# Softmax weights that go through memory undivided, with their reciprocals as a tenth block

## The chip, the cores and the metric

The kernel runs on one core of one Trainium2 chip. The metric is the device time of one execution in microseconds. Engines are named as in the profile: PE (TensorE, matmuls), PEld (its weight loads), DVE (VectorE), ACT (ScalarE), POOL (GpSimd), SP (SyncE, which here issues all DMAs). A step below is one turn of the kernel's main loop.

## The reference

Attention with 8 batches, 8 heads, 576 rows and a head width of 64, all f32, in which each row keeps only its 32 largest scores, followed by a layer with a hidden width of 2048:

```python
scores = scale * np.matmul(q, k.transpose(0, 1, 3, 2))
kth = np.partition(scores, -top_k, axis=-1)[..., -top_k:-top_k + 1]
scores = np.where(scores >= kth, scores, -1000000000.0)
scores = scores - np.max(scores, axis=-1, keepdims=True)
attn = np.exp(scores)
attn = attn / (np.sum(attn, axis=-1, keepdims=True) + 1e-09)
x = np.matmul(attn, v)              # then heads side by side: (4608, 512)
h = x @ w_in                        # (4608, 2048)
g = np.where(h >= 1, h, np.where(h <= -1, 0.0, (h + 1) ** 2 / 4))
out = g @ w_out                     # (4608, 512)
```

## The kernel before, in words

A step takes two heads (a head pair `hp`) of one block `t` of 128 queries: rows of 576 scores for each head, 128 queries on the partitions. 576 is four blocks of 128 (NT = 4) and a tail of 64; the tail queries of two heads fill one step (`t == NT`). There are 144 steps, 128 of them with `t < NT` and 16 tails. Four steps (two for tails, of two batches together) fill a chunk of 128 rows of x, held transposed in `xT` (128 x 4 x 128, one part for each head pair), and each of the 36 chunks goes through the hidden layer.

What a step does:

- `scores` (L329): PE multiplies queries and keys into PSUM (`sp`), ACT copies them to `s` with the scale (L348).
- `first_top` and `weights` (L371, L406): DVE finds the 32nd largest of each row. It works on the larger of each pair of columns (`more`) and the smaller (`less`, both L361), with rounds of max8 and match_replace (L368, L381, L409 and so on), and merges the two lists with a scan (L440). ACT takes exponentials of all scores (L384). At the end DVE zeroes the exponentials below the threshold and sums the rest (L447: out e, sums z).
- `divide` (L391), at the start of the next step: DVE takes the reciprocals of z (L393). Then either (`by_tensor`, in the first 9 steps and the last two) ACT makes diagonal matrices of them (L397), or POOL multiplies the 128 x 576 weights of each head by them (L400).
- The weights must be transposed for the value product. `by_tensor` steps do it on PE (`transpose_w`, L456). The other 133 go through memory (`move_w`, L473): ACT sorts the f32 weights into their upper and lower 16-bit halves (L477, two copies), SP writes them to DRAM (L479, `rows`) and then issues a DMA transpose back into `wT` (L480), which is 9 blocks of 128 x 128: four for each head and one with both tails. SP's transpose waits until the rows have landed.
- `values` (L486), two steps later: PE multiplies values and `wT` into the PSUM tile `po` (L494, L502 for tails), and ACT copies it into the step's part of `xT` (L507, L509).
- When the last part of a chunk is there, `mlp` (L518) queues its work: 8 groups `hidden` (L521; each 8 products `ph`, L527, of which every fourth reads `xT[:, 3]`; then ACT L531 and L538, then POOL L543, L544, L545), and 16 products `final` (L547; `py`, L550), each group's four groups behind it. The output `y` is copied by ACT (L553) and written (L555).

Keys and queries of the later batches are transposed in the same way as weights, by ACT (`turn`, L272), a write to DRAM (L274, `lines`) and a DMA transpose (L275). ACT also inspects the loaded weights of the layer in odd steps (L168).

What sets the order: PE, DVE, ACT and POOL carry out their instructions in the order in which the loop (L723) emits them. Each step has 7 slots. The division of the step before is emitted in slot 0, `transpose_w` of the step before in slot 1, the value product of the step two before in slot 2, followed by the scores of the step two ahead; `move_w` of the step before comes in slot 3. After every slot `advance` (L621) takes queued work of the layer by a planner's cost, so that each step gets an even share of it. SP's order is not in that list; the framework sets it.

Buffers that matter here: `halves` has one buffer, `wT` three, `ph` and `po` share three in PSUM, `r` has two, `g` eight, the queries `q_in` two and the tail queries `q_tl` one.

Of the kernel before, what the change touches and what calls it, by code (L numbers as in the profile page):

```python
# [11 lines left out]
F32 = mybir.dt.float32  # L12
U16 = mybir.dt.uint16
# [3 lines left out]
ALU = mybir.AluOpType  # L17
# [8 lines left out]
def kernel(  # L26
# [10 lines left out]
    nc = tc.nc  # L37
    B, H, S, D = q.shape
    NTOK, DM = out.shape
    DFF = moe_w_in.shape[1]  # L40
    P = 128
# [4 lines left out]
    NT = S // P  # L46
    SM = NT * P
    TL = S - SM
    assert 2 * TL == P
    SH = S // 2  # L50
    BLOCKS = 2 * NT + 1
# [120 lines left out]
    def run(ctx, paired):  # L172
        xtp = ctx.enter_context(tc.tile_pool(name="xtp", bufs=6))
        stage = ctx.enter_context(tc.tile_pool(name="stage", bufs=2))
        att = ctx.enter_context(tc.tile_pool(name="att", bufs=2))
        dram = ctx.enter_context(tc.tile_pool(name="dram", bufs=3, space=bass.MemoryType.DRAM))
# [3 lines left out]
        def whole(x, b):  # L180

            return x[b, :, 0:SM, :].rearrange("h (p c) d -> p h c d", c=NT)
# [17 lines left out]
        def load_queries(b, t):  # L200
            if t < NT:
                q_in = stage.tile([P, H, D], F32, name="q_in", bufs=2)
                nc.sync.dma_start(out=q_in, in_=whole(q, b)[:, :, t, :])
            else:
                q_in = stage.tile([TL, H, D], F32, name="q_tl", bufs=1)
                nc.sync.dma_start(out=q_in, in_=q[b, :, SM:S, :].rearrange("h p d -> p h d"))
            return q_in


        def main(i):  # L210
            return slice(0, SM) if i == 0 else slice(TL, S)

        def tail(i):
            return slice(SM, S) if i == 0 else slice(0, TL)

        def part(i, j):
            return slice(0, TL) if i == j else slice(TL, P)
# [171 lines left out]
                st["rest"] = att.tile([P, 2, S], F32, name="rest", bufs=1)  # L389

        def divide(st):  # L391
            rz = att.tile([P, 2], F32, name="rz")
            nc.vector.reciprocal(rz, st["z"])  # L393
            if st["by_tensor"]:
                st["rz"] = diag = (late or words).tile([P, 2, P], F32, name="diag", tag="halves", bufs=1)
                for i in range(2):
                    nc.scalar.activation(diag[:, i, :], ident, AF.Copy, scale=rz[:, i:i + 1])  # L397
            else:
                for i in range(2):
                    nc.gpsimd.tensor_scalar(st["e"][:, i, :], st["e"][:, i, :], rz[:, i:i + 1], 1.0, ALU.mult, ALU.mult)  # L400
            if paired:
                m, seconds, kth = st["m"], st["seconds"], st["kth"]
                nc.gpsimd.tensor_tensor(out=excess[:, 2 * m:2 * m + 2], in0=seconds[:, 8:9 + SPLIT:SPLIT], in1=kth[:, LAST:7:-SPLIT],
                                        op=ALU.subtract)

        def weights(st, before, after):  # L406
            m, tops = st["m"], st["tops"]
            for x in largest(st, 8):
                x()  # L409
                if before is not None:  # L410
                    divide(before)
                    before = None
# [38 lines left out]
            if after is None:  # L451
                divide(st)
# [2 lines left out]

        def transpose_w(st):  # L456
            w = st["e"]
            st["wT"] = wT = (late or words).tile([P, BLOCKS, P], F32, name="wT", bufs=3 if late else 1)
            pt = ps.tile([P, 2, NT, P], F32, name="pw", tag="a", bufs=2)
            for i in range(2):  # L460
                for c in range(NT):
                    nc.tensor.matmul(pt[:, i, c, :], w[:, i, main(i)][:, c * P:(c + 1) * P], st["rz"][:, i, :],  # L462
                                     start=True, stop=True)
            for i in range(2):
                nc.scalar.copy(wT[:, i * (NT + 1):i * (NT + 1) + NT], pt[:, i])
            pt = ps.tile([P, P], F32, name="pwt", tag="a", bufs=2)
            for i in range(2):
                nc.tensor.matmul(pt[i * TL:(i + 1) * TL, :], w[:, i, tail(i)], st["rz"][:, i, :], start=True, stop=True)
            nc.scalar.copy(wT[:, NT], pt)
# [1 line left out]


        def move_w(st):  # L473
            st["wT"] = wT = late.tile([P, BLOCKS, P], F32, name="wT", bufs=3)
            halves = late.tile([P, 2, 2 * S], U16, name="halves")
            for i in range(2):
                nc.scalar.copy(halves[:, :, i * S:(i + 1) * S], st["e"][:, i, :].bitcast(U16).rearrange("p (k t) -> p t k", t=2))  # L477
            rows = dram.tile([P, 2, 2 * S], U16, name="rows")
            nc.sync.dma_start(out=rows, in_=halves)  # L479
            nc.sync.dma_start_transpose(wT.bitcast(U16), rows.rearrange("p t k -> (p t) k"))  # L480

        def block(i, c):
            return i * (NT + 1) + c if c < NT else NT


        def values(st):  # L486
            t, hp, v_in, v_tl = st["t"], st["hp"], st["keys"]["v"], st["keys"]["v_tl"]
            wT = st["wT"]
            po = ps.tile([P, P], F32, name="po", tag="ph", bufs=3)
            if t < NT:  # L490
                for c in range(NT + 1):
                    for j in range(2):
                        h = 2 * hp + j
                        nc.tensor.matmul(po[j * D:(j + 1) * D], v_in[:, h, c, :] if c < NT else v_tl[0][:, h, :],  # L494
                                         wT[:, block(j, c)], start=(c == 0), stop=(c == NT))
            else:
                for i in range(2):
                    cols = slice(i * TL, (i + 1) * TL)
                    for c in range(NT + 1):
                        for j in range(2):  # L500
                            h = 2 * (hp + i) + j
                            nc.tensor.matmul(po[j * D:(j + 1) * D, cols], v_in[:, h, c, :] if c < NT else v_tl[1][:, h, :],  # L502
                                             wT[:, block(i, c), part(i, j)],
                                             start=(c == 0), stop=(c == NT))
            xT, col = st["xT"]
            if t < NT:
                nc.scalar.copy(xT[:, hp, col:col + P], po)  # L507
            else:
                nc.scalar.copy(xT[:, hp:hp + 2, col:col + TL], po.rearrange("p (i n) -> p i n", i=2))  # L509

# [68 lines left out]
        for b, t in rounds:  # L579
            tile_of = (b, t) if t < NT else (b - b % 2, t)  # L580
            ch = chunks.index(tile_of)
            col = TL if t == NT and b % 2 else 0
            for hp in (range(NHP) if t < NT else range(0, NHP, 2)):
                steps.append((b, t, hp, ch, col))
        n = len(steps)
# [5 lines left out]
        words, late = conversion.enter_context(tc.tile_pool(name="words", bufs=1)), None  # L591
# [53 lines left out]
        def fetch(i):  # L645
            if i < len(rounds) and rounds[i] not in q_ins:
                q_ins[rounds[i]] = load_queries(*rounds[i])
# [63 lines left out]
        def values_until(m):  # L711
            nonlocal valued, pe_time
            while valued < min(m, n):
                pe_time = max(pe_time, ready_at[valued]) + 1.25
                values(state[valued])
                state[valued] = None
                if valued in ready:
                    ch = ready[valued]
                    mlp(xTs[ch], rows_of(*chunks[ch]), mlp_pool, ch == len(chunks) - 1)
                valued += 1  # L720

        first_late = None
        for m in range(n + 2):  # L723
# [3 lines left out]
            elif not early and late is None:  # L727
                conversion.close()
                room.clear()
                late = ctx.enter_context(tc.tile_pool(name="late", bufs=1))  # L730
# [15 lines left out]
            for slot in range(SLOTS):  # L746
# [11 lines left out]
                if slot == 1 and 1 <= m <= n and state[m - 1]["by_tensor"]:  # L758
                    pe_time = max(pe_time, done[m - 1] + 2.0) + 1.0
                    transpose_w(state[m - 1])  # L760
                    ready_at[m - 1] = pe_time + 1.8
                if slot == 3 and 1 <= m <= n and state[m - 1] is not None and not state[m - 1]["by_tensor"]:
                    move_w(state[m - 1])
                    ready_at[m - 1] = done[m - 1] + 15.0
# [75 lines left out]
```

## Time and profile before

| | |
|---|---|
| median of 3 runs (lowest to highest) | 1533.05 us (1530.18 to 1536.14) |
| the profiled execution | 1536.15 us |
| its span, first to last instruction | 1534.3 us |
| granted TensorE clock, mean | 0.979 |
| POOL L400, the division: 266 instructions | 250.2 us busy, 951 ns each |
| ACT L477, the halves: 266 instructions | 293.6 us busy, 1144 ns each |
| DVE L447, threshold and sum: 288 instructions | 267.3 us busy, 962 ns each |
| rows to DRAM, 133 times 576 KB | 3.2 us from issue to landing |
| transpose of the rows, 133 times | 5.0 us from issue to landing |
| DMA share, mean rate | 64.7% of 16 engines, 169 GB/s |

In the lines of the profile, a group or a row of the timeline has engine, line, operation and tiles (out<-in). A line of waits has the waiting instruction, what released it, the sum in us, how many times, and the longest. In the timeline the first two numbers are the start (us from the span's start) and the length; `[0.90 <-ACT g L538]` says that the engine was idle for 0.90 us before it, until ACT's L538 released it. Times in the table by stage are busy times of the engines, which overlap.

### The profile page before, as it was taken

What the parts mean: (1) busy time and instruction counts of PE and PEld (TensorE: products, weight loads), DVE (VectorE), ACT (ScalarE), POOL (GpSimd) and SP (SyncE); (2) the same over time, 40 slices, a digit from 0 to 9 for tenths busy, and PEclk for the clock granted to TensorE, in tenths of its full rate; (3) what the DMA queues carried; (4) which work ended last, traced back from release to release, by engine and by line L of the source; (5) the groups of instructions that cost most, each with busy time, mean ns of one, the idle gap of its engine ahead of it and who ended that gap; (6) DMA issues with size and microseconds to landing.
All of it is one profiled execution on the core that took longest, in us unless ns stands there. A gap on an engine that the chain in (4) does not pass through costs nothing.

```text
span 1534.3 us, 32263 instructions
## 1 busy us (share of the span) xinstructions
PE 1452.4 (95%) x10625; PEld 1043.3 (68%) x10625; DVE 1445.1 (94%) x4443; ACT 1160.6 (76%) x2269; POOL 977.1 (64%) x1382
## 2 busy tenths in 40 slices
PE   5587999999999999999999999999999999999998
PEld 3465677677777767677777777676676677777675
DVE  6998999999999999999999999999999999999912
ACT  5776877877778888788778887787777888777732
POOL 4887556666666666566666666666666666666630
PEclk7788999999999999999999999999999999999999
DMA  8532467875676866986677877886577767565410
GB/s 241 158 116 81 121 167 157 214 190 158 165 196 183 214 171 180 217 215 179 165 196 185 202 176 186 212 204 178 155 182 193 197 167 191 156 160 157 134 39 17
DMA packets 512450, 259.78 MB, mean 169 GB/s; under 512 B 459152, under 2 KB 467344, under 8 KB 512272
## 3 DMA queue, kind: packets, MB, share of 16 engines
q1 hardware_dynamic: 512272, 257.62, 64.7%
q8 instruction: 86, 1.41, 0.4%
q14 instruction: 92, 0.75, 0.2%
HBM read 62.91 MB, written 102.04 MB: 108 GB/s over the span
## 4 chain that ended last, share of the span: by engine, by line
PE 79%; ACT 6%; DVE 6%; DMA 5%; issue 2%; POOL 1%; SPq 0%; DVEq 0%; ACTq 0%; POOLq 0%
PE py L550 30%; PE ph L527 28%; PE sp L347 9%; PE po L494 9%; DMA wT<-rows 2%; ACT halves L477 2%; DMA rows<-halves 2%; ACT e L384 1%; PE po L502 1%; DVE more L368 1%; DVE bits L148 1%; DVE e L447 1%; ACT raw L168 1%; PE pw L462 1%; ACT s L348 1%
## 5 line engine op out<-in xcount | busy, mean ns | idle before, releaser
L527 PEld LDWEIGHTS ph<-xT,w_in 128*128 128x128 f32 x4608 | 549.0, 193 | 102.8 <-issue 82.6
L527 PE MATMUL ph<-xT,w_in 128*128 128x128 f32 x4608 | 559.1, 277 | 4.5 <-POOL w_in L161 4.5
L550 PE MATMUL py<-w_out,g 128*128 128x512 f32 x1152 | 551.3, 603 | 0.0
L543 POOL TENSOR_SCALAR r<-r 128x256 f32<-128x256 f32 x276 | 152.1, 551 | 432.0 <-ACT r L531 431.9
L368 DVE MATCH_REPLACE8 more<-tops,more 128x288 f32<-128x288 f32 x864 | 374.9, 437 | 0.0
L550 PEld LDWEIGHTS py<-w_out,g 128*128 128x128 f32 x1152 | 198.5, 191 | 182.0 <-issue 161.8
L477 ACT COPY halves<-e 128x1152 uint16<-128x1152 uint16 x266 | 293.6, 1144 | 17.7 <-POOL e L400 8.3
L447 DVE SCALAR_TENSOR_TENSOR e<-s,kth,e 128x577 f32<-128x577 f32 x288 | 267.3, 962 | 1.8 <-ACT e L384 1.6
L545 POOL TENSOR_TENSOR g<-r,g 128x256 f32<-128x256 f32 x280 | 244.3, 873 | 22.0
L400 POOL TENSOR_SCALAR e<-e,rz 128x576 f32<-128x576 f32 x266 | 250.2, 951 | 3.6 <-DVE rz L393 3.6
L531 ACT ACTIVATE r<-ph,half 128x256 f32<-128x256 f32 (+1 forms) x296 | 136.4, 461 | 121.3 <-PE ph L527 84.4
L384 ACT ACTIVATE e<-s,nmax 128x576 f32<-128x576 f32 x288 | 222.7, 774 | 4.7
L348 ACT ACTIVATE s<-sp 128x576 f32<-128x576 f32 x288 | 172.6, 653 | 47.2 <-PE sp L347 45.2
L544 POOL TENSOR_TENSOR r<-r 128x256 f32<-128x256 f32 x276 | 190.7, 691 | 23.0
L347 PE MATMUL sp<-kT,qT 64*128 64x288 f32 x1024 | 163.8, 437 | 11.9 <-ACT kT L250 11.0
L494 PEld LDWEIGHTS po<-wT,v_in 128*64 128x64 f32 x2048 | 111.3, 137 | 83.3 <-ACT g L538 33.7
L494 PE MATMUL po<-wT,v_in 128*64 128x128 f32 x2048 | 143.6, 280 | 20.4 <-DMA wT<-rows 10.6
L538 ACT ACTIVATE g<-ph,minus 128x256 f32<-128x256 f32 x280 | 130.5, 466 | 0.0
L361 DVE TENSOR_TENSOR less<-s 128x576 f32<-128x576 f32 x144 | 125.9, 874 | 0.0
L409 DVE MAX8 tops<-more 128x8 f32<-128x288 f32 x288 | 125.4, 443 | 0.0
L347 PEld LDWEIGHTS sp<-kT,qT 64*128 64x128 f32 x1024 | 90.2, 189 | 48.1 <-issue 15.6
L361 DVE TENSOR_TENSOR more<-s 128x576 f32<-128x576 f32 x144 | 112.6, 782 | 6.7 <-ACT s L348 6.7
(91 smaller groups left out, 1423.6 us busy)
## 6 DMA issues: line engine op xcount, KB each, us to landing
rows<-halves SPq DMA_DIRECT2D x133, 576.0 KB, 3.2
lines<-parts SPq DMA_DIRECT2D x48, 256.0 KB, 2.8
q_in<-in_q_dram SPq DMA_DIRECT2D x32, 256.0 KB, 4.3
kT<-in_moe_w_in_dram SPq DMA_DIRECT2D x32, 256.0 KB, 3.3
v_in<-in_moe_w_out_dram SPq DMA_DIRECT2D x32, 256.0 KB, 3.0
v_in<-in_v_dram SPq DMA_DIRECT2D x32, 256.0 KB, 4.1
raw<-in_moe_w_in_dram SPq DMA_DIRECT2D x32, 256.0 KB, 3.1
out_dram<-y SPq DMA_DIRECT2D x32, 256.0 KB, 3.1
```

Source lines behind the costliest of these rows:

```text
L347: nc.tensor.matmul(*x, start=True, stop=True)
L361: nc.vector.tensor_tensor(out=x, in0=s[:, :, 0:SH], in1=s[:, :, SH:S], op=op)
L368: nc.vector.match_replace(out=st["rest"][:, i, :], in_to_replace=eight(st["tops"], i, r - 8), in_values=src[:, i, :], imm_value=LOWEST)
L384: nc.scalar.activation(e[:, i, :], s[:, i, :], AF.Exp, bias=nmax[:, i:i + 1])
L400: nc.gpsimd.tensor_scalar(st["e"][:, i, :], st["e"][:, i, :], rz[:, i:i + 1], 1.0, ALU.mult, ALU.mult)
L447: nc.vector.scalar_tensor_tensor(out=st["all"][1][:, i, :], in0=st["all"][0][:, i, :], scalar=last[i], in1=st["all"][1][:, i, :], op0=ALU. ...
L477: nc.scalar.copy(halves[:, :, i * S:(i + 1) * S], st["e"][:, i, :].bitcast(U16).rearrange("p (k t) -> p t k", t=2))
L494: nc.tensor.matmul(po[j * D:(j + 1) * D], v_in[:, h, c, :] if c < NT else v_tl[0][:, h, :], wT[:, block(j, c)], start=(c == 0), stop=(c == ...
L527: nc.tensor.matmul(ph[:, i], w_in[:, kk, f * P:(f + 1) * P], xT[:, kk], start=(kk == 0), stop=(kk == NK - 1))
L544: nc.gpsimd.tensor_tensor(out=r, in0=r, in1=r, op=ALU.mult)
L545: nc.gpsimd.tensor_tensor(out=g, in0=r, in1=g, op=ALU.add)
L550: nc.tensor.matmul(py[0], gs[f // group][:, f % group], w_out[:, f, :], start=(f == 0), stop=(f == NF - 1))
```

## The change

The weights of the 117 steps that go through memory and are no tails are not divided before they go. Instead their two reciprocals a row, spread over 64 columns each, are appended as 128 more columns; they come back transposed as a tenth block of `wT`, in which the upper 64 partitions hold the reciprocals of one head and the lower 64 those of the other, one column for each query. That is the layout of the value product, and POOL multiplies the part of `xT` by that block, after ACT has copied it from PSUM. Tails are divided as before; their rows are as long as before, but lie in tiles with room for 128 more columns.

`rz` gets three buffers, since it is read a step later than before. `wT` and `halves` grow. The tail queries share the two buffers of the other queries.

```diff
                 q_in = stage.tile([P, H, D], F32, name="q_in", bufs=2)
...
-                q_in = stage.tile([TL, H, D], F32, name="q_tl", bufs=1)
+                q_in = stage.tile([TL, H, D], F32, name="q_tl", tag="q_in", bufs=2)
...
         def divide(st):
-            rz = att.tile([P, 2], F32, name="rz")
+            rz = att.tile([P, 2], F32, name="rz", bufs=3)
             nc.vector.reciprocal(rz, st["z"])
             if st["by_tensor"]:
...
+            elif st["t"] < NT:
+                st["rz"] = rz
             else:
                 for i in range(2):
                     nc.gpsimd.tensor_scalar(st["e"][:, i, :], st["e"][:, i, :], rz[:, i:i + 1], 1.0, ALU.mult, ALU.mult)
...
         def move_w(st):
-            st["wT"] = wT = late.tile([P, BLOCKS, P], F32, name="wT", bufs=3)
-            halves = late.tile([P, 2, 2 * S], U16, name="halves")
+            st["wT"] = wT = late.tile([P, BLOCKS + 1, P], F32, name="wT", bufs=3)
+            halves = late.tile([P, 2, 2 * S + P], U16, name="halves")
             for i in range(2):
                 nc.scalar.copy(halves[:, :, i * S:(i + 1) * S], st["e"][:, i, :].bitcast(U16).rearrange("p (k t) -> p t k", t=2))
-            rows = dram.tile([P, 2, 2 * S], U16, name="rows")
-            nc.sync.dma_start(out=rows, in_=halves)
-            nc.sync.dma_start_transpose(wT.bitcast(U16), rows.rearrange("p t k -> (p t) k"))
+            n = 2 * S
+            if st["t"] < NT:
+                n += P
+                nc.scalar.copy(halves[:, :, 2 * S:n].rearrange("p t (i d) -> p t i d", d=D),
+                               st["rz"].bitcast(U16).rearrange("p (i t) -> p t i", t=2).unsqueeze(3).to_broadcast([P, 2, 2, D]))
+            rows = dram.tile([P, 2, 2 * S + P], U16, name="rows")
+            nc.sync.dma_start(out=rows[:, :, 0:n], in_=halves[:, :, 0:n])
+            nc.sync.dma_start_transpose(wT[:, 0:n // P].bitcast(U16), rows[:, :, 0:n].rearrange("p t k -> (p t) k"))
...
             if t < NT:
                 nc.scalar.copy(xT[:, hp, col:col + P], po)
+                if not st["by_tensor"]:
+                    x = xT[:, hp, col:col + P]
+                    nc.gpsimd.tensor_tensor(out=x, in0=x, in1=wT[:, BLOCKS, :], op=ALU.mult)
```

## The prediction

> **What bounds the kernel now.** I read four views: the page's busy times, busy time by stage, the waits of PE and of DVE from 200 to 1463 us, and the timeline around two places where PE meets the changed work.
>
> First the page, then the stages (columns: us, then busy time of PE, PEld, DVE, ACT, POOL, the granted clock, DMA share, GB/s):
>
> ```profile
> PE 1452.4 (95%) x10625; PEld 1043.3 (68%) x10625; DVE 1445.1 (94%) x4443; ACT 1160.6 (76%) x2269; POOL 977.1 (64%) x1382
> ```
> ```profile
> 200.00:400.00 200.00, 196.00 (x1530) 141.99 (x1527) 200.00 (x620) 156.48 (x302) 129.43 (x182) 1.00 0.70 179
> ...
> 1000.00:1200.00 200.00, 195.46 (x1387) 139.73 (x1386) 194.88 (x608) 157.61 (x300) 130.07 (x180) 1.00 0.70 182
> 1200.00:1400.00 200.00, 199.64 (x1544) 141.90 (x1543) 199.01 (x618) 159.70 (x308) 134.05 (x187) 1.00 0.66 174
> 1400.00:1463.00 63.00, 60.88 (x417) 41.90 (x417) 62.83 (x192) 45.46 (x83) 42.13 (x61) 1.00 0.52 142
> 1463.00:1535.00 72.00, 63.73 (x413) 46.08 (x409) 10.60 (x37) 22.45 (x61) 12.28 (x22) 0.98 0.06 18
> ```
>
> Both PE and DVE look full, so the waits must say who follows whom. Of PE, then of DVE, both from 200 to 1463 us:
>
> ```profile
> PE po L494 <- DMA wT<-rows: 8.1, 5, 3.3
> PE po L494 <- ACT g L538: 6.0, 7, 1.2
> PE pw L462 <- ACT diag L397: 2.1, 1, 2.1
> PE sp L347 <- DMA qTt<-lines: 2.0, 2, 1.6
> PE po L502 <- DMA wT<-rows: 1.0, 1, 1.0
> ```
> ```profile
> DVE more L361 <- ACT s L348: 6.7, 9, 1.6
> DVE e L447 <- ACT e L384: 1.6, 2, 1.4
> ```
>
> PE waits 19.2 us in 1263, and DVE's few waits are for `s`, which ACT copies from PE's scores: DVE runs ahead and meets PE. Step by step the trace says the same: from the reciprocal of a step (L393) to its value product (L494) it is 18 us at step 12 and 32 at step 93. So PE, with a fixed list of work, sets the end; when DVE is done (1463 us) PE still has 64 us of work. A change is worth what it does to PE's 19 us of waits, or adds to them. They are of two kinds: weights that come late (`wT<-rows`), and a PSUM buffer that ACT has not yet emptied (`ACT g`).
>
> **The change, part by part.** 133 steps send weights through memory; 16 of them are tails (t = NT) and keep their division, 117 change.
>
> 1. *POOL loses the division.* 234 of the 266 L400 go, at 951 ns: 222 us. Who gains? (a) DVE. L447 takes 0.80 us at best and 0.962 in the mean of 288, and the long ones lie over a POOL instruction; matching the two in the trace, 25 us of DVE's excess lies over an L400, some 22 over those removed. DVE then gets further ahead of PE, and this is worth 0 to the end; were DVE the bound, it would be 22 us, but no more than PE's 19 us of waits could come back. (b) ACT, whose halves wait for L400 18 times, 8.3 us in all, up to 0.6 each. Nearly all lie where the weights land 1 us or more early. I take -1.
>
> 2. *ACT gains a broadcast copy*, 256 uint16 a partition, behind the two copies of L477. The nearest row: 1152 elements take 1144 ns and 1024 (L272) 1040, so 0.81 ns each, and 256 come to 0.42 us. No row has a broadcast source; bounds are L507 (128 x f32, 0.27) and L531 (256 x f32, 0.47). In all 117 x 0.42 = 49 us on an engine that is busy 79% of a step; most of it takes the place of waits for PE. Once a chunk it does not: PE runs three groups `ph` in a row, and `po` then needs the buffer that ACT empties only behind halves:
>
> ```profile
> 1040.41 2.19 ACT L477 COPY halves<-e 128x1152 uint16<-128x1152 uint16 x2
> 1042.51 0.77 ACT L384 ACTIVATE e<-s,nmax 128x576 f32<-128x576 f32 x1
> 1043.18 0.45 ACT L531 ACTIVATE r<-ph,half 128x256 f32<-128x256 f32 x1
> 1043.54 0.46 ACT L538 ACTIVATE g<-ph,minus 128x256 f32<-128x256 f32 x1
> ...
> 1044.05 1.09 PE L494 MATMUL po<-wT,v_in 128*64 128x128 f32 x16 [0.90 <-ACT g L538]
> ```
>
> The product starts 0.05 us after `g` ends. Going through all 30 such places: in 11 that move a changed step there is no slack, so each pays 0.42; in 15 `po` starts 0.40 after `g`, 0.35 of it slack, so each pays 0.07; 4 belong to tails. 11 x 0.42 + 15 x 0.07 = **5.7 us** (with 0.27: 3.0; with 0.47: 7.0).
>
> 3. *Weights arrive later.* Rows grow from 576 to 640 KB. 256 KB (`lines`) land in 2.8 us and 576 in 3.2: +0.08. The transpose lands in 3.4 us for 4 blocks (`kT`) and 5.0 for 9: +0.32 for one more, and SP's issue goes from 1.26 to 2.62 us over those 5 blocks: +0.27, behind which wait the loads and the next rows. With ACT's 0.42 the weights come 0.82 us later. The median step has 2.7 us between landing and product, so it pays nothing. But in 14 changed steps they land less than 0.5 us ahead (10, 12, 20, 21, 43, 49, 50, 56, 57, 84, 92, 99, 120, 141), mostly where SP also loads keys and turns them. Neighbours pay once: 11 places at 0.82 less some 0.15 of slack = **7.4 us**. Bounds: nothing, if SP's queue falls otherwise; 18 us if the tenth block costs double and each step pays for itself.
>
> 4. *POOL multiplies xT before the hidden layer.* A 128x256 add of two tiles (L545) takes 732 ns and 128x2 (L403) 197, so 128x128 is 0.46 us. It is on the path only where a chunk begins, 28 times, and there at once:
>
> ```profile
> 709.31 1.09 PE L494 MATMUL po<-wT,v_in 128*64 128x128 f32 x16
> ...
> 710.18 2.47 POOL L400 TENSOR_SCALAR e<-e,rz 128x576 f32<-128x576 f32 x2
> ...
> 710.67 0.27 ACT L507 COPY xT<-po 128x128 f32<-128x128 f32 x1 [2.11 <-PE po L494]
> 710.75 1.29 DVE L447 SCALAR_TENSOR_TENSOR e<-s,kth,e 128x577 f32<-128x577 f32 x1
> ...
> 711.73 2.05 PE L527 MATMUL ph<-xT,w_in 128*128 128x128 f32 x16
> ```
>
> `xT` is there at 710.94, `ph` starts 0.79 later; but only its fourth product (kk = 3, 0.67 on) reads the last part, so cover is 1.46 us. In the other chunks it is the same within 0.1, but for four where POOL ends its `g` up to 0.4 us after `xT`. Against it stands DVE's L447, which runs at that moment from 590 us on. Alone the product needs 0.05 + 0.46; behind one whole L447 (0.81) 1.32, still covered. The longest POOL instructions say it can be worse: L545 goes from 0.73 to 2.07, 1.34 longer; then 1.85, 0.4 late. I take a stall in a few chunks, **2 us** (bounds 0 and 28 x 0.4 = 11). What waits behind the product on POOL are later r and g, which PE reads four groups later.
>
> [...]
>
> 5. *The query buffer.* Tail queries take the shared tag: the same loads, each waiting for a buffer that was turned just before. Nothing; if SP's order shifts with it, that is inside term 3's bounds.
>
> Sum: -1 + 5.7 + 7.4 + 2 = +14.1 us. The profiled execution took 1536.15 us (span 1534.3 and 1.85 around it), so it would be 1550; the median of the three runs, 1533.05, lies 3.1 below it, so the forecast there is **1547**.
>
> **Rivals.** *It is all hidden* (1533, within 7.7): stalls absorb each other, since a PE that waits for weights gives ACT time, and the buffer wait of that chunk disappears. For it: PE waits only 19 us now, so most of its work has cover. Against: the buffer wait recurs every 39 us at equal slack, and a product that starts as soon as the buffer is free can hide none of 0.42 more. *It is faster* (about 1521): DVE's 22 us count, because PE's 8 us of late weights and its waits on ACT are in truth late divisions on POOL, so that weights leave earlier than now. It decides where halves wait for L400 in steps whose weights come just in time; there 0.5 us of ACT's wait goes and pays for the new copy, and up to 12 of PE's 19 us vanish. Against: 18 such waits, hardly any in the 14 late steps. *The product is late* (about 1563): POOL's multiply stands behind r and g and two L447, PE waits 0.8 us at each of 28 chunk starts, 22 us in place of 2, less 4 of buffer waits that this relieves.
>
> **How the numbers follow.** About 0.5% (7.7 us) is what a measurement here can tell from no change. Forecast 0.54, product late 0.15, hidden 0.21, faster 0.10. Slower by over 0.5%: 0.54 + 0.15, about 0.69; same 0.21; faster 0.10. The range reaches from 1526 (part of the faster case; PE's waits for late weights gone) to 1570 (term 3 at 18 and term 4 at 11 with term 2 at 7 give 1569), leaving out some 0.06 at each end.
>
> **What would show it.** POOL's busy time some 165 us lower; L447's mean nearer 0.87; DVE's busy time some 20 us lower but its waits for `s` longer by as much. The new ACT copy at 0.42. PE's waits from 200 to 1463: for `wT<-rows` from 9 to about 16 us, for `ACT g` from 6 to about 11, and a new line with L527 behind POOL's product of 0 to 5. The landing of the transpose at 5.3. I am wrong if PE's waits stay at 19 us, if the new line is the largest, or if PE's work itself changes (its busy time should stay within 5 us of 1452).

## The result and the profile after

The changed kernel takes 1546.80 us (median of 5 runs, 1543.19 to 1550.69) against 1533.05; the ratio is 1.009 with a 95% interval of 1.0066 to 1.0114. Its profiled execution took 1550.69 us with a span of 1548.9, so 14.6 us more than the profiled execution before. The forecast was 1547, and 1550 for the profiled execution. The sum was right; three of its terms were not: one was too small, two too large, and they made up for each other.

The busy times and the stages, as before the change (us, then PE, PEld, DVE, ACT, POOL, clock, DMA share, GB/s):

```profile
PE 1460.6 (94%) x10625; PEld 1047.1 (68%) x10625; DVE 1442.4 (93%) x4443; ACT 1191.8 (77%) x2386; POOL 815.8 (53%) x1265
```
```profile
200.00:400.00 200.00, 193.94 (x1502) 140.66 (x1501) 196.10 (x617) 158.93 (x314) 105.36 (x160) 0.99 0.71 186
...
1000.00:1200.00 200.00, 192.19 (x1342) 136.59 (x1343) 189.01 (x589) 157.36 (x311) 101.00 (x158) 0.98 0.74 193
...
1463.00:1550.00 87.00, 75.89 (x481) 53.54 (x479) 24.74 (x80) 30.39 (x77) 17.89 (x33) 0.98 0.14 41
```

POOL lost 161 us (165 in the forecast). PE is busy 8.2 us longer at the same number of instructions, so it was slower at times: the clock column says so, 0.98 and 0.99 where it stood at 1.00. (2.3 of the 8.2 fall in the first 160 us, which the change doesn't touch.) PE's waits, then DVE's, from 200 to 1463 us:

```profile
PE po L501 <- DMA wT<-rows: 9.5, 4, 3.5
PE po L501 <- ACT g L548: 8.8, 11, 1.2
PE ph L537 <- POOL xT L517: 3.9, 4, 1.9
PE sp L347 <- DMA qTt<-lines: 3.0, 2, 1.5
```
```profile
DVE more L361 <- ACT s L348: 16.1, 22, 3.4
DVE e L449 <- ACT e L384: 8.4, 10, 2.4
```

Waits for weights stay where they were (8.1 + 1.0 before), those for ACT's `g` grow by 2.8, and POOL's product makes a new line with 3.9 us in only four places. DVE now waits three times as long (24.5 us against 8.3) for what ACT makes of PE's scores, so its lead buys nothing.

The two new instructions, POOL's product and ACT's copy (count, busy us, mean ns, then idle time before them):

```profile
L517 POOL TENSOR_TENSOR xT<-xT,wT 128x128 f32<-128x128 f32 x117 | 67.1, 574 | 17.2 <-ACT xT L514 17.1
...
L483 ACT COPY halves<-rz 128x256 uint16<-128x256 uint16 x117 | 46.7, 399 | 0.0
```

**Where the 14.6 us come from.** Lining up the 144 value products of both traces, most steps have the same distance from the one before to a few hundredths of a us. The difference grows in jumps: 3.85 at step 16, and 0.91 to 0.97 at steps 52, 88 and 124 (6.6 together: the first tail step of each pair of batches); 0.28 to 0.31 at nine places, one a chunk, from step 97 to 133 (2.7); 2.8 at steps 56 and 57 and 1.5 at 92 and 93, after waits for weights; 1 each at 12 and 86; 0.6 at 140 and 141; some jumps back by 0.1 to 0.8 sum to -2.4. The start, which the change doesn't touch, took 0.8 longer in this execution. Seen from PE: its waits from 160 us on are 8.7 us longer, and it spends 10.2 us more at half clock (3.4 at 246 us, 3.4 at 649, 6.8 at 1000, against one stretch of 3.4 at 993 before), which costs 5.1. With the 0.8 that is 14.6.

**The jump of 0.9 at the tails.** The timeline of the changed kernel at step 51, the last before the tails:

```profile
595.69 2.46 POOL L402 TENSOR_SCALAR e<-e,rz 128x576 f32<-128x576 f32 x2
596.11 0.27 ACT L514 COPY xT<-po 128x128 f32<-128x128 f32 x1 [2.10 <-PE po L501]
...
597.13 0.94 PE L537 MATMUL ph<-xT,w_in 128*128 128x128 f32 x6
...
598.12 0.19 POOL L405 TENSOR_TENSOR excess<-seconds,kth 128x2 f32<-128x2 f32 x1
598.27 0.45 POOL L517 TENSOR_TENSOR xT<-xT,wT 128x128 f32<-128x128 f32 x1
...
598.77 1.38 PE L537 MATMUL ph<-xT,w_in 128*128 128x128 f32 x10 [0.70 <-POOL xT L517]
```

`xT` is there at 596.38, but POOL is dividing the tail's weights (two L402, 2.46 us in all: 1.24 and 1.23 us beside DVE's L449, where those with neither L449 nor L361 beside them take 0.75), and the product comes behind it. PE starts the hidden group, gets to its fourth product and waits 0.70 us. (The loop emits a step's value product three turns later, not two as the description above has it, so the division ahead of it in the queue is that of the second tail step.) The waits at the later tails are like it, 0.64 and 0.65. At the first, at 245.73 us, it is 1.92 us: there the product came 2.53 us after `xT` and itself took 1.04 us, beside L449 (0.45 in the lines above). The clock follows:

```profile
242.70:246.10 3.40, 1.48 (x11) 1.12 (x10) 3.40 (x14) 3.37 (x6) 2.98 (x4) 1.00 0.85 174
246.10:249.50 3.40, 3.40 (x13) 2.37 (x12) 3.40 (x13) 2.09 (x4) 1.01 (x1) 0.51 0.62 210
249.50:253.00 3.50, 3.50 (x22) 2.54 (x21) 3.50 (x13) 0.00 (x0) 3.34 (x5) 0.99 0.48 99
```

PE was busy 1.48 of the 3.4 us up to 246.1, and the next 3.4 us were granted 0.51. So that one wait cost 1.92 us and, with the slower stretch behind it, 1.9 more.

**The jump of 0.3 a chunk.** ACT's copy stands in the burst that the prediction showed:

```profile
1051.15 2.19 ACT L479 COPY halves<-e 128x1152 uint16<-128x1152 uint16 x2
1053.25 0.40 ACT L483 COPY halves<-rz 128x256 uint16<-128x256 uint16 x1
1053.55 0.77 ACT L384 ACTIVATE e<-s,nmax 128x576 f32<-128x576 f32 x1
...
1054.58 0.45 ACT L548 ACTIVATE g<-ph,minus 128x256 f32<-128x256 f32 x1
...
1055.09 1.09 PE L501 MATMUL po<-wT,v_in 128*64 128x128 f32 x16 [1.19 <-ACT g L548]
```

The wait was 0.90 before and is 1.19 now. The copy takes 0.40 us, but the instruction behind it starts 0.1 before it ends, as the copy itself does behind the halves, so the burst grows by 0.30.

### The profile page after: what moved, and what is told of

Its sections match the earlier page's. It is cut to its first block, busy times and chain, and to the rows that moved or that the text cites. A ratio compares the mean times of both kernels' runs of the same rounds, so it can differ in the third digit from the quotient of the medians.

```text
span 1548.9 us, 32485 instructions
## 1 busy us (share of the span) xinstructions
PE 1460.6 (94%) x10625; PEld 1047.1 (68%) x10625; DVE 1442.4 (93%) x4443; ACT 1191.8 (77%) x2386; POOL 815.8 (53%) x1265
## 4 chain that ended last, share of the span: by engine, by line
PE 63%; DVE 18%; ACT 8%; DMA 5%; issue 3%; POOL 2%; SPq 1%; POOLq 0%; DVEq 0%; ACTq 0%
PE py L560 24%; PE ph L537 21%; PE po L501 8%; PE sp L347 8%; DVE more L368 4%; DVE e L449 3%; ACT halves L479 2%; DMA wT<-rows 2%; DMA rows<-halves 2%; ACT e L384 1%; DVE tops L411 1%; DVE tops L430 1%; DVE seconds L437 1%; DVE tops L419 1%; DVE more L361 1%
## 5 line engine op out<-in xcount | busy, mean ns | idle before, releaser
L449 DVE SCALAR_TENSOR_TENSOR e<-s,kth,e 128x577 f32<-128x577 f32 x288 | 264.9, 952 | 8.5 <-ACT e L384 8.4
L555 POOL TENSOR_TENSOR g<-r,g 128x256 f32<-128x256 f32 x280 | 236.8, 846 | 22.0
L554 POOL TENSOR_TENSOR r<-r 128x256 f32<-128x256 f32 x276 | 198.1, 718 | 23.0
L361 DVE TENSOR_TENSOR more<-s 128x576 f32<-128x576 f32 x144 | 111.3, 773 | 16.1 <-ACT s L348 16.1
L411 DVE MAX8 tops<-more 128x8 f32<-128x288 f32 x288 | 125.4, 443 | 0.0
L347 PEld LDWEIGHTS sp<-kT,qT 64*128 64x128 f32 x1024 | 90.8, 190 | 48.8 <-issue 17.5
L361 DVE TENSOR_TENSOR less<-s 128x576 f32<-128x576 f32 x144 | 120.7, 838 | 0.0
L381 DVE MAX8 tops<-more 128x8 f32<-128x288 f32 x288 | 116.3, 443 | 0.0
```

Source lines behind the costliest of these rows:

```text
L347: nc.tensor.matmul(*x, start=True, stop=True)
L361: nc.vector.tensor_tensor(out=x, in0=s[:, :, 0:SH], in1=s[:, :, SH:S], op=op)
L449: nc.vector.scalar_tensor_tensor(out=st["all"][1][:, i, :], in0=st["all"][0][:, i, :], scalar=last[i], in1=st["all"][1][:, i, :], op0=ALU. ...
L554: nc.gpsimd.tensor_tensor(out=r, in0=r, in1=r, op=ALU.mult)
L555: nc.gpsimd.tensor_tensor(out=g, in0=r, in1=g, op=ALU.add)
```

## The experiments

Theory A: PE is the bound, and the change costs what it adds to PE's waits: POOL's product at the four tails, with one loss of the clock (some 6 us); ACT's copy in a burst once a chunk (some 3); the tenth block's longer way (the rest). Rival B: the product is held off everywhere by DVE's two-input instructions (L449 and L361: in the changed kernel's trace L517 takes 0.45 us in the median of the 87 places with neither beside it, 0.97 in the 24 beside L449 and 0.97 in the 6 beside L361 alone). Rival C: the terms as forecast, ACT 5.7, block 7.4, product 2. e1 to e4, e5 to e8, e9 with e10, and e11 with e12 each have their own runs of the kernel before (medians 1535.37, 1533.75, 1535.76, 1531.40), so only ratios are compared. In what follows, a difference of two ratios is given in us by their middles; the intervals leave some 3 to 6 us either way.

| run | median us | ratio to before, 95% interval |
|---|---|---|
| the change | 1546.80 | 1.0090 (1.0066 to 1.0114) |
| e1 change, division kept ahead of tails | 1541.66 | 1.0049 (1.0030 to 1.0067) |
| e2 before + ACT's copy | 1537.00 | 1.0006 (0.9988 to 1.0023) |
| e3 before + tenth block, shared buffers | 1538.48 | 1.0014 (0.9995 to 1.0033) |
| e4 change without the product | 1541.74 | 1.0044 (1.0025 to 1.0063) |
| e5 before without the division | 1533.72 | 0.9996 (0.9981 to 1.0010) |
| e6 e1, POOL spreads the reciprocals | 1552.70 | 1.0120 (1.0083 to 1.0157) |
| e7 e6, POOL splits one head too | 1563.21 | 1.0184 (1.0157 to 1.0212) |
| e8 before + shared buffers | 1529.28 | 0.9973 (0.9955 to 0.9991) |
| e9 e8, inspection in even turns | 1528.27 | 0.9954 (0.9938 to 0.9969) |
| e10 e1, inspection in even turns | 1533.57 | 0.9998 (0.9986 to 1.0011) |
| e11 before + longer rows, shared buffers | 1533.08 | 1.0008 (0.9991 to 1.0025) |
| e12 e8 again | 1532.05 | 0.9996 (0.9983 to 1.0010) |

**e1: the steps ahead of a tail keep their division**

```diff
-            elif st["t"] < NT:
+            elif st["later"]:
                 st["rz"] = rz
...
+                state[m]["later"] = (not state[m]["by_tensor"] and steps[m][1] < NT
+                                     and not (m + 1 < n and steps[m + 1][1] == NT))
```
(The conditions in `move_w` and `values` are changed likewise.)

> The changed kernel, but the four steps just ahead of a tail step keep their division on POOL and get no product after it. Theory A (from the two traces): of the 14 us that the change costs, some 6 come from these four places, where POOL's product stands in its queue behind the tail's own division (L402, twice), so that the first hidden group waits 0.65 to 1.9 us, and once the granted clock falls to half for 3.4 us after it. Then PE's waits for POOL's product go from 3.9 us to under 0.3, and the time to 1541 to 1543. Rival B: the product is late because DVE's two-input instructions hold POOL off; then only a third of the waits goes and the time stays within 2 us of the changed kernel (1545 to 1547).

1.0049, so 0.0041 or 6.3 us came back (2 to 11 by the intervals; in the profiled execution of the change the four waits were 3.9 us and the loss of the clock 1.9). PE's waits from 200 to 1463 us:

```profile
PE po L501 <- ACT g L548: 9.5, 11, 1.9
PE po L501 <- DMA wT<-rows: 8.3, 3, 3.5
PE sp L347 <- DMA qTt<-lines: 1.9, 1, 1.9
PE po L501 <- ACT r L541: 0.3, 1, 0.3
```

The line of POOL's product is gone, and so is the half clock at 246 us. Theory A holds here: four steps of 117 made nearly half of the loss. Rival B falls: the product is still there in the other 25 chunks, under the same DVE instructions, and no longer delays PE. (The four steps also lose ACT's copy and the tenth block; e4, which keeps both, shows that this is not what counts.)

**e4: no product**

```diff
-                if not st["by_tensor"]:
-                    x = xT[:, hp, col:col + P]
-                    nc.gpsimd.tensor_tensor(out=x, in0=x, in1=wT[:, BLOCKS, :], op=ALU.mult)
```

> The changed kernel with POOL's product left out, so that the output lacks the division. Theory A: PE's four waits for it (3.9 us) and one half-clock stretch go, 1541. Forecast's term 2 us: 1545. Rival: the product is on the path in every chunk by what it does to r and g behind it on POOL, 1537 or less.

1.0044, the same as e1 within the intervals: without any product one gets as much as without the four late ones. So the product's price, some 6 to 7 us, is at the tails.

The product could also cost by its place behind PE: a buffer of `wT` is free only when POOL has read its tenth block. But SP's transposes wait as long without the product: what PE or POOL released held them back for 182 us in the kernel before, 200 in the changed one and 200 in e4.

**e2: ACT's copy alone**

```diff
+            if st["t"] < NT:
+                spare = late.tile([P, 2, P], U16, name="spare")
+                nc.scalar.copy(spare.rearrange("p t (i d) -> p t i d", d=D),
+                               st["rzs"].bitcast(U16).rearrange("p (i t) -> p t i", t=2).unsqueeze(3).to_broadcast([P, 2, 2, D]))
             rows = dram.tile([P, 2, 2 * S], U16, name="rows")
```

> The kernel before, with ACT's broadcast copy of the reciprocals added behind the two halves, into a tile that nothing reads. Theory A: it costs 0.29 at the ten places where a value product waits for the last PSUM buffer, 3 us in all, and nothing where there was 0.35 of slack: 1536. Forecast's term 2: 5.7 us, 1539. Rival: ACT has room, 1533.

1.0006: 0.9 us, between a gain of 1.8 and a loss of 3.5. In its profile PE's waits for `g` grew from 6.0 to 9.4 us, as theory A has it; those for weights and for `qTt` fell by 2.3, and no stretch of half clock lies in the middle of that execution. The term of 5.7 is out of the interval; whether it is 3 or 1 stays open.

**e3: the tenth block alone**

```diff
+            if not kept:
+                kept.append(late.tile([P, 2, 2 * S + P], U16, name="halves"))
+                nc.gpsimd.memset(kept[0][:, :, 2 * S:2 * S + P], 0)
+            halves = kept[0]
...
+            n = 2 * S + (P if st["t"] < NT else 0)
+            rows = dram.tile([P, 2, 2 * S + P], U16, name="rows")
+            nc.sync.dma_start(out=rows[:, :, 0:n], in_=halves[:, :, 0:n])
+            nc.sync.dma_start_transpose(wT[:, 0:n // P].bitcast(U16), rows[:, :, 0:n].rearrange("p t k -> (p t) k"))
```
(It has the shared query buffers, without which it doesn't fit, and a buffer of its own for `diag`, which shares one with `halves` in the kernel before.)

> The kernel before, with 128 more columns in the rows and a tenth block in the transpose (zeros that are written once and never used) and the shared query buffers; the division stays. Forecast's term 3 without ACT's part (0.40 of 0.82 us later, 11 places): about 3 us, 1536. Theory A: rows and transpose land 0.3 to 0.5 us later, but PE's waits for the weights grow by 1 us at most, unless one of them passes some 3 us and the clock falls after it (1.7 us each time): 1533 to 1537. Rival: SP's queue is the real cost, 1540 or more.

1.0014, 2 us over the kernel before. Rows land after 3.4 us and the transpose after 5.2, as in the changed kernel (3.2 and 5.0 before), and PE's waits for weights are 10.4 us from 200 to 1463 against 9.1. Against the shared buffers alone (e8 and e12, 0.9973 and 0.9996; waits for weights 6.6 and 7.0 us) the block costs 3 to 6 us by the middles, and from nothing to some 10 by the intervals.

**e8 and e12: the shared query buffers alone**

```diff
-                q_in = stage.tile([TL, H, D], F32, name="q_tl", bufs=1)
+                q_in = stage.tile([TL, H, D], F32, name="q_tl", tag="q_in", bufs=2)
```

> The kernel before with only the two kinds of query tiles in shared buffers. Theory A and the forecast's part 5: nothing, 1533 to 1536, PE's waits within 2 us in sum. Rival: SP's order around the tails is what makes the weights late there, and it moves with the buffers: PE's waits at 640 and 990 us change by over 1 us, and the time by 3 or more.

0.9973, 4 us faster. The order of the instructions is the same on PE, DVE, ACT and POOL; on SP 560 of the 776 places in the order hold another DMA: the query loads, the moves of weights and the loads of layer weights have moved. PE's waits for `qTt` and `wT` from 200 us on are 6.6 us instead of 11.1. It was run again:

> The kernel before with only the shared query buffers, again, on the same chip as the run beside it. Theory A (SP's order around the tails): again 0.997 of the kernel before. Rival: the earlier 0.9973 was chance, 1.000.

0.9996. The two intervals overlap only from 0.9983 to 0.9991, so the first result was partly chance, and the buffers are worth 1 to 3 us, if anything. The shorter waits came again (7.0 us), but in that execution PE spent 10.2 us at half clock after 160 us, the last microseconds aside, against 6.8 in e8's and 3.4 in the kernel before. That they cost nothing, as forecast, holds; that they gain is not settled.

**e5: no division**

```diff
-            else:
+            elif st["t"] == NT:
                 for i in range(2):
                     nc.gpsimd.tensor_scalar(st["e"][:, i, :], st["e"][:, i, :], rz[:, i:i + 1], 1.0, ALU.mult, ALU.mult)
```

> The kernel before with POOL's division left out in the steps that are no tails (so that the output lacks it) and nothing put in its place: what the removal alone is worth. Theory A: PE is the bound, so DVE's 20 us of shorter instructions turn into waits for s, and the time falls by the forecast's 1 us or not at all: 1531 to 1536. Rival (the forecast's faster case): the weights leave earlier, PE's 12 us of waits for them shrink to a half, 1527 or less.

0.9996: what the change removes, 222 us of POOL's time, is worth 0.6 us, between 2.9 gained and 1.5 lost. POOL's busy time falls to 751.9 us and DVE's from 1445.1 to 1433.4, and both are off the path. Theory A; the rival, from which a faster kernel was to come, falls.

**e6 and e7: POOL in ACT's place**

```diff
             elif st["later"]:
-                st["rz"] = rz
+                st["halves"] = halves = late.tile([P, 2, 2 * S + P], U16, name="halves")
+                nc.gpsimd.tensor_copy(halves[:, :, S:2 * S], st["e"][:, 1, :].bitcast(U16).rearrange("p (k t) -> p t k", t=2))
+                nc.gpsimd.tensor_copy(halves[:, :, 2 * S:2 * S + P].rearrange("p t (i d) -> p t i d", d=D),
+                                      rz.bitcast(U16).rearrange("p (i t) -> p t i", t=2).unsqueeze(3).to_broadcast([P, 2, 2, D]))
```
(e7 has both copies, e6 the second alone; ACT's instructions for the same columns are left out of `move_w`.)

> The changed kernel with the four steps ahead of a tail divided as before, and with the reciprocals spread by POOL, in the place where it divided, and not by ACT. Against the run with the tails' cure alone it takes 0.40 us off ACT's burst. Theory A: PE's waits for ACT's g fall from 9.5 to about 6 us as before the change, 1537 to 1539. Rival: ACT's copy costs nothing at the end, 1541 to 1542. A third outcome: POOL waits for the single halves buffer, which rows of the step before still read, and the time rises.

1.0120, 11 us worse than e1: the third outcome. In the waits of all engines, and of PE from 200 to 1463 us:

```profile
POOL halves L400 <- DMA rows<-halves: 120.9, 49, 8.4
```
```profile
PE ph L537 <- POOL xT L517: 11.2, 10, 2.2
```

The waits for ACT's `g` fell to 5.2 us, as theory A said. But POOL now waits 49 times, up to 8.4 us, until the rows of the step before have left the one halves buffer, and behind it stands the product that a chunk needs at once.

> As the run before it, and POOL also splits the second head's weights into halves (L477's second copy, 1.14 us on ACT), in the place where it divided. Theory A (what bounds is PE, which waits for ACT's burst once a chunk and for weights that leave late): ACT's burst is 1.5 us shorter, PE's waits for ACT's g go below 2 us and those for weights fall by a third, 1525 to 1531, faster than the kernel before. Rival: POOL gets to the split as late as it got to the division (9 us after the reciprocal in the middle, 15 in every fourth step), so rows wait for it, and POOL's two-byte copy is slow: 1535 or more.

1.0184. The two lines again:

```profile
POOL halves L400 <- DMA rows<-halves: 96.6, 39, 10.1
```
```profile
PE ph L538 <- POOL xT L518: 23.8, 18, 3.4
```

No wait of PE for `g` is left in that window, so the shorter burst does what theory A said; but POOL's copy takes 1.30 us on top of the same wait, and the product is late in 18 places. It ends on the rival's side, though not by its wait: POOL doesn't come too late to the split, it stands too long before it, at the buffer.

**e9 and e10: the inspection in even turns**

```diff
-                    if m % 2:
+                    if m % 2 == 0:
                         inspect()
```

> The kernel before with the shared query buffers, and with the inspection of the loaded weights (two ACT instructions of 0.72 us with their reads, L168) moved from odd turns of the loop to even ones; the burst behind which a value product waits for ACT's g is in odd turns. Theory A (the ten places are a collision of ACT's inspection, halves and exponential in one turn a chunk): PE's waits for ACT's g fall from 6 us to under 1, and the time to about 0.3% under that with the shared buffers alone, a ratio to the kernel before of 0.994. Rival: the burst only moves to another turn, 0.997.

0.9954 (0.9938 to 0.9969): a version that beats both kernels. Against the shared buffers alone (e8, e12) that is 3 to 6 us. The waits for ACT's `g` are gone (one of 1.1 us for `r`, which reads the same buffers, is new); what is left between 200 and 1463 us is mostly weights:

```profile
PE po L494 <- DMA wT<-rows: 9.2, 7, 3.8
PE po L502 <- DMA wT<-rows: 3.8, 2, 2.8
```

> The changed kernel with the cure for the tails' four places and the inspection in even turns. Theory A: PE's waits for ACT's g fall from 9.5 us to about 1, so that ACT's 0.40 us costs nothing; what is left against the same version of the kernel before is the tenth block's longer way, some 4 to 6 us: a ratio to the kernel before of 0.998 to 1.000. Rival: ACT's copy is late for the weights as well, 1.003 or more. Should it be under the run beside it, the change is worth having once its two collisions are gone.

0.9998: 7.8 us under e1, with no wait for `g` either (two for `r`, 2.0 us). With both collisions cured the change is as fast as the kernel before, and 6.7 us slower than the same cure without the change (e9).

**e11: the longer rows without the tenth block**

```diff
-            nc.sync.dma_start_transpose(wT[:, 0:n // P].bitcast(U16), rows[:, :, 0:n].rearrange("p t k -> (p t) k"))
+            nc.sync.dma_start_transpose(wT[:, 0:BLOCKS].bitcast(U16), rows[:, :, 0:2 * S].rearrange("p t k -> (p t) k"))
```
(The lines of e3, with this one in place of its last.)

> The kernel before with the shared query buffers and with rows of 640 KB written (128 more columns, zeros), but only the first nine blocks transposed back: the half of the tenth block that is SP's write. Theory A: of the block's price against the shared buffers alone (some 6 us) the greater part is the transpose's (issue 0.27 us longer on SP, landing 0.3 later, against 0.1 to 0.2 for the rows), so this is within 2 us of the run beside it. Rival: SP's transpose waits for the rows, so it is their landing that counts, and this is 4 us or more above it.

1.0008 against 0.9996 beside it: 1.8 us, within what the intervals leave open. It fits theory A, but PE's waits for weights are 10.6 us, as long as with the tenth block (10.4 in e3) and longer than without it (6.6 and 7.0). So which of the two halves costs is not shown; the block's parts can't be told apart at this size.

## Why the prediction was right, point by point

- **PE is the bound, and DVE's and POOL's gains are worth nothing**: right (e5). The detail was wrong: DVE's busy time was to fall by 20 us and fell by 2.7, with L449's mean at 952 ns in place of 870. The division left, but other POOL instructions came to lie under the same DVE instruction. Of its time above 0.80 us each, by the POOL instruction that lies longest beside it, 20.3 of 46.7 us lay over a division before; after, 43.9 are left, 8.3 over the product and 10.0 over the subtraction L405 (1.4 before). In e5, with no product, 41.9 are left, now mostly over r and g, and DVE's busy time falls by 11.7.
- **Term 2, ACT's copy (5.7)**: the mechanism was right, the place too, the price 0.40 us for 0.42. It was mis-sized: the waits for `g` grew by 2.8. The copy adds 0.29 to a wait, not 0.42, at the ten late places, and the 15 places with 0.35 of slack pay nothing, since 0.29 fits in it.
- **Term 3, late weights (7.4)**: the mechanism was right, the size too large. Rows and transpose land 0.2 us later each (forecast 0.08 and 0.32), and the median step has 2.2 us between landing and product where it had 2.7. The 14 steps without slack were taken to stay, but the shared query buffers changed SP's order, and two effects met: the buffers alone cut PE's waits for weights from 9.1 to 6.6 and 7.0 us (e8, e12), and with nearly that order the change, e1, e3 and e4 have 8.3 to 10.4. So the sum grew by 0.4 us only, and the block itself costs 3 to 6 us (e3). Two long waits, 3.21 and 3.52 us, were each followed by half clock (before it was one), which was in no term; e8 and e12 have such stretches too, so that the block brings them is not shown.
- **Term 4, the product (2)**: the step that failed. The cover of 1.46 us was right for 25 of the chunks (29 begin with a product, not 28), where the product makes PE wait for less than 0.15 us each. It was read from places where an L400 stood in POOL's queue and was taken to go; ahead of a tail it stays, and the product is behind it. There it cost some 6 to 7 us (e1, e4). The 1.34 us by which L545 was longer, and from which the stall was worked out, did not come with the product: L517 takes 456 ns in the median and 1043 at most, 0.59 more, less than one L449 alone (0.80).
- **Part 5, the buffers (nothing)**: they cost nothing, as forecast; a gain of up to 3 us is open.
- **The sum**: +14.1 against 13.75 in the medians. Product 4 to 5 too low, copy and weights together 4 to 9 too high: that the sum came out within the interval of the ratio, 10.1 to 17.5 us, is luck as much as working.
- **What would show it**: the copy (0.40 us for 0.42), the waits for `g` (8.8 for 11), the product's line (3.9, within 0 to 5) and the transpose's landing (5.2 for 5.3) came as forecast; the waits for weights (9.5 for 16) and L449's mean did not. And one sign of being wrong came: PE's busy time was to stay within 5 us of 1452 and rose by 8.2, mostly by half clock, which the prediction had left out.

## What to carry to other kernels

Follow the bound engine's waits, not busy time: here 161 us taken off GpSimd were worth nothing, and 0.40 us added to ScalarE cost 0.29 in every chunk in which TensorE already waited for it. When work is put at the end of an engine's queue and its result is needed at once, go through every place where it is needed and ask what stands ahead of it there after the change; the exceptions (here the tails, which keep the old path) are where it is late. A collision that recurs once in a period is best cured by moving something else out of that turn: one changed parity gained 3 to 6 us (e9 against e8 and e12), while leaving the division out altogether gained 0.6 (e5).

## What the runs showed of the hardware that was not expected

One wait of TensorE in the changed kernel cost twice its length, 1.92 us and 1.9 more; others as long cost no more than themselves. In the traces before and after, the granted clock stands at 1.00 or at 0.50. The stretches at 0.50, 11 before and 12 after, last 3.41 us or a multiple of it (the one that the end cuts off aside), and within a trace they begin whole multiples of 3.413 us apart, to 0.001 of that length: 246.14, 648.91 and 1000.49 us in the changed kernel are 118.0 and 103.0 such lengths from each other. Both traces can be cut into pieces of that length, counted from where a stretch begins. Of the 772 pieces at full clock between 160 and 1490 us, four had PE busy for 0.44 of their length or less: 0.09 before (at 989.23 us), 0.44, 0.32 and 0.37 after (242.73, 645.50 and 997.07). Half clock followed each of the four, and none of the others, which had PE busy for 0.45 or more. The length of a wait alone doesn't tell, though the expectation of e3 speaks of some 3 us: the wait of 1.92 us at 243.8 lay in one piece (busy 0.44) and lost the clock, another of 1.92 us in the same execution, at 207.2, lay across two (0.60 and 0.83) and didn't, and one of 3.51 us in e1 (from 990.53) didn't either. Its two pieces and the next, in the columns of the stages:

```profile
988.78:992.19 3.41, 1.75 (x10) 0.92 (x9) 3.41 (x13) 3.41 (x6) 0.00 (x0) 1.00 0.69 138
992.19:995.61 3.42, 1.57 (x22) 1.40 (x24) 3.42 (x13) 0.58 (x2) 2.70 (x3) 1.00 0.79 172
995.61:999.02 3.41, 3.41 (x19) 2.00 (x16) 3.18 (x9) 1.78 (x5) 0.46 (x1) 1.00 0.61 221
```

Seen from the span's start the pieces lie differently in the two traces (they begin 0.81 of a length past a whole number of them in the kernel before, 0.11 in the changed one), so the loss at 246 us may be that execution's alone; there is one trace of the changed kernel. What makes the clock fall is not shown.

SP's order of DMAs is not written in the program, and a change that seems to have nothing to do with it can move it: sharing a buffer (e8) put another DMA in 560 of SP's 776 places and changed no other engine's order, while leaving out the division (e5) moved none. PE's waits for weights, 9.1 us before, were 6.6 and 7.0 with the shared buffers (e8, e12), but 5.8 in e5 as well, where the order stayed, and so comparisons of single terms under 3 us stayed open.
